# The last two dK stores of a cached-attention backward kernel, each as sixteen transfers of 8 partitions

## The chip, the core and the metric

The kernel runs on one core of a Trainium2 chip. A core has four compute engines (PE for matmuls, DVE for elementwise work, ACT, POOL), a fifth one, SP, that does nothing here but issue transfers, and sixteen DMA engines, which move all data between HBM and the on-chip memory of 128 partitions. The metric is the device time of one execution in microseconds, as the median of several runs.

## The reference

What is computed is a decoding step with its gradients: layer norm, attention over a cache of 4,096 keys and values for 4 x 32 heads, a gated MLP, and the derivative by eight of the inputs. Cut to what matters here:

```python
B, Sq, D = 4, 1, 512
H, Sk, Dh = 32, 4096, 128
"k_cache": (B, H, Sk, Dh), "v_cache": (B, H, Sk, Dh)      # bf16
...
q = ((x @ wq).reshape(B, Sq, H, Dh)).transpose(0, 2, 1, 3)
scores = jnp.einsum("bhqd,bhkd->bhqk", q, k_cache) * (Dh ** -0.5)
p = softmax(scores)
o = jnp.einsum("bhqk,bhkd->bhqd", p, v_cache)
...
_out, _vjp = jax.vjp(_f, A_x, A_k_cache, A_v_cache, A_wq, A_wo, B_w1, B_w3, B_w2)
return (_out, *_vjp(grad_out))
```

With one query per head, the gradient of a head's values is an outer product, dV = p dO^T, and that of its keys is dK = dS q^T, with dS the gradient of the scores. Each is 4,096 x 128 numbers in bf16, 1 MiB a head. The caches are read (K once, V twice) and two arrays of their size are written, which makes up nearly all of the 705 MB that the kernel moves.

## The kernel before

**Stages.** The forward part goes through the 128 heads with K and V. The backward part then goes through them again with V alone. Its first 32 heads are done one by one, the other 96 in 48 pairs (`NT = 48`; `t` is the pair). A pair is two heads side by side: each head takes 64 partitions, and each partition holds 64 rows of 128 numbers, 16,384 bytes that are contiguous in HBM as well (`two_heads`, L1272).

**One pair.** `load_pair` (L1276) loads V, `front_pair` (L1292) transposes it on PE and ACT and multiplies it with dO, `group_dS_pair` (L1319) makes dS, and `grad_pair` (L1386) makes and stores one result: it takes a pair of slots, lets DVE write the outer product into it (`outer_pair`, the instruction at L1379), has SP store it (L1389), and gives the slots back. dV (`out_3`) comes from `more_V` (L1395), which runs ahead by some heads, and dK (`out_2`) from the loop over `t` at the end of the kernel. So the last stores of the program, in SP's order, are dV and dK in turn, then dV of the last pair, dK of pair `NT-2`, dK of pair `NT-1`. There is no load behind them.

**Slots.** All these tiles are pieces of one on-chip tile, `arena`, of 23 slots; `Slot2` (L146) takes two neighbouring ones, those that were given back longest ago. The program's dependencies are found by the framework from the pieces that each instruction reads and writes; the order of instructions on each engine is the order in the source.

**The queue.** SP runs its list in order. An instruction that waits holds up all behind it. Every transfer of SP's counts up one of eight semaphores, which the framework hands out in turn, so a semaphore comes back with every eighth transfer. In the built program each transfer waits for what it reads or overwrites, and also until the earlier transfer of its own semaphore has landed in full: all its parts, on all DMA engines. In the program of before, the last two dK stores wait, besides DVE's product, for the eighth transfer before each.

**A landing** is the time at which the last of a transfer's sixteen parts (one for each DMA engine) has been counted. A 128-row store of a pair puts 8 rows, so 8 packets of 16,384 bytes, on each DMA engine.

Of the kernel before, what the change touches and what calls it, by code (L numbers as in the profile page):

```python
# [27 lines left out]
def kernel(  # L28
# [22 lines left out]
    nc = tc.nc  # L51
# [6 lines left out]
    Dh = A_k_cache.shape[3]  # L58
# [6 lines left out]
    SJ = Sk // P  # L65
# [142 lines left out]
    for i in range(2):  # L208
        t = fcon.tile([P, 64], BF16, name=f"onesw{i}")
# [4 lines left out]
    def ones_window(col):  # L214
# [11 lines left out]
                          in_=rowg[:, None, :, None].to_broadcast([P, 4, 8, 4]))  # L226
# [738 lines left out]
    with ExitStack() as c2:  # L965
# [297 lines left out]
        NT = (NH - SP) // 2  # L1263
# [8 lines left out]
        def two_heads(ap, t):  # L1272
            b, h = t % B, H0 + t // B * 2
            return ap[b, h:h + 2].rearrange("h (p j) d -> (h p) (j d)", p=P // 2)
# [103 lines left out]
        def outer_pair(dst, col2, row):  # L1378
            nc.vector.tensor_tensor(  # L1379
                out=dst.rearrange("p (j r t) -> p j r t", r=Dh // 2, t=2),  # L1380
                in0=col2[:, :, None, :].to_broadcast([P, 2 * SJ, Dh // 2, 2]),
                in1=row.rearrange("p (r t) -> p r t", t=2)[:, None, :, :].to_broadcast([P, 2 * SJ, Dh // 2, 2]),
                op=ALU.mult,
            )

        def grad_pair(out_ap, t, col2, row):  # L1386
            g_ = Slot2()
            outer_pair(g_.t[:, 0:2 * SJ * Dh], col2, row)
            nc.sync.dma_start(out=two_heads(out_ap, t), in_=g_.t[:, 0:2 * SJ * Dh])  # L1389
            g_.give()  # L1390

        O0, S0, S1, L, LP = 2, 21, 35, 5, 3
        gvd = {"n": 2, "t": 0}
# [1 line left out]
        def more_V(upto):  # L1395
            while gvd["n"] < min(SP, upto):
                s = gvd["n"]
                P_pairs(s)
                replicate("rdo", s - s % REP)
                grad_V(s)  # L1400
                P_pairs(s + 1)
                P_pairs(s + 2)
                gvd["n"] += 1
                if s % REP == 2 and s + 2 < SP:
                    replicate("rdo", s + 2)
                elif s % REP == 2:
                    replicate_pair("rdo", 0)
                if s >= SP - 2:
                    P2_pair(s - SP + 2)
            while gvd["t"] < NT and SP + 2 * gvd["t"] + 2 <= upto:  # L1410
                t = gvd["t"]
                P2_pair(t)
                replicate_pair("rdo", t // B)
                grad_pair(out_3, t, pP2.pop(t), reps["rdo", "p", t // B][:, t % B, :])
                P2_pair(t + 1)
                gvd["t"] += 1
                if t % B == 2:
                    replicate_pair("rdo", t // B + 1)
# [57 lines left out]
        for t in range(NT):  # L1476
            s = SP + 2 * t
            load_pairs(t + LP)
            if t % B == 2:
                replicate_pair("rq", t // B + 1)  # L1480
            if t + LP < NT:
                front_pair(t + LP, lambda: side(s))
            else:
                if t + LP == NT:
                    rows_out()
                    rows_T()
                side(s)
            more_V(s + 2 + lead_V(s))
            grad_pair(out_2, t, pdS[t // 2][:, t % 2], reps["rq", "p", t // B][:, t % B, :])
            if t % 2 == 1 and t + 1 < NT:  # L1490
                group_dS_pair((t + 1) // 2)
            side(s + 1)
# [31 lines left out]
```

## Time and profile before

| what | value |
|---|---|
| median of 3 runs | 1698.76 us (1698.05 to 1699.05) |
| span of the profiled execution | 1696.2 us |
| moved by DMA | 707.45 MB, mean 417 GB/s |
| DVE, PE, ACT, POOL busy | 1234.4, 1233.4, 959.5, 336.9 us |
| 2,048 KB stores (dV and dK of pairs) | 96, median 27.9 us from issue to landing |
| outer product of a pair on DVE (L1379) | 4.42 us |
| last dV store: issued, landed | 1658.14, 1685.22 us |
| dK store of pair NT-2: issued, landed | 1662.52, 1690.05 us |
| dK store of pair NT-1: issued, landed | 1666.81, 1694.89 us |

Times within the execution count from its first instruction. Busy times are sums over the span, and engines run side by side, so they don't add up to it. The time from issue to landing is mostly queueing: several stores stand in the queues at a time. The profiled execution's span is 2.6 us less than the median of the runs, which count a little before and behind it.

### The profile page before, as it was taken

The numbers are of one execution on the slowest core, as the hardware profiler recorded it, in microseconds if no ns is written. First come the engines' busy times: TensorE is split into PE (matmuls) and PEld (weight loads), VectorE is DVE, ScalarE is ACT, GpSimd is POOL, SyncE is SP. The second block draws the span as 40 slices with busy tenths as digits, with TensorE's granted clock in tenths as the row PEclk, the third lists the DMA queues.
The fourth block names the chain that finished last, engine by engine and source line by source line (L and its number), as shares of the span: only waits on it lengthen the run. The fifth ranks groups of instructions, "written<-read, shape, count | busy, mean of one in ns | idle before, by whom it ended". The sixth has DMA issues, their size and how long they took to land.

```text
span 1696.2 us, 37839 instructions
## 1 busy us (share of the span) xinstructions
PE 1233.4 (73%) x16228; PEld 943.4 (56%) x16228; DVE 1234.4 (73%) x1198; ACT 959.5 (57%) x1490; POOL 336.9 (20%) x583
## 2 busy tenths in 40 slices
PE   5889888888888888877876755667665666766650
PEld 4777667666677666655655544444444444444440
DVE  5989999999998997667766466575665655655683
ACT  3555544454454544677665555666665666666650
POOL 1211222222222222222231121011210102011120
PEclk8999999999999999899898689886678777676675
DMA  9999999999999999999999999999999999999995
GB/s 401 424 424 424 424 424 424 424 424 423 416 423 406 424 414 397 395 414 425 425 425 429 428 429 428 429 430 429 429 429 428 418 430 429 422 418 425 415 429 230
DMA packets 81000, 707.45 MB, mean 417 GB/s; under 512 B 8748, under 2 KB 12984, under 8 KB 15296
## 3 DMA queue, kind: packets, MB, share of 16 engines
q1 hardware_dynamic: 80416, 704.94, 99.0%
q8 instruction: 127, 2.08, 0.5%
q14 instruction: 41, 0.34, 0.0%
q0 software_dynamic: 416, 0.10, 0.0%
HBM read 422.59 MB, written 282.34 MB: 416 GB/s over the span
## 4 chain that ended last, share of the span: by engine, by line
DMA 46%; DVE 9%; PE 3%; issue 2%; ACT 1%; DVEq 0%; POOL 0%; SPq 0%; ACTq 0%
DMA out_dram<-arena 43%; DVE arena L1379 7%; DMA arena<-in_A_v_cache_dram 3%; DVE arena L806 1%; PE M_ps L472 1%; DVE arena L457 1%; PE pt_w L601 0%; ACT arena L1299 0%; ACT Pn L436 0%; DVEq L1519 0%; PE kP_ps L482 0%; DVE dPr L1326 0%; PE pt_tps L1298 0%; PE gu_ps L873 0%; PE dn_ps L904 0%
## 5 line engine op out<-in xcount | busy, mean ns | idle before, releaser
L1299 ACT COPY arena<-pt_tps 128x1024 bf16<-128x1024 bf16 x384 | 369.8, 1023 | 232.3 <-PE pt_tps L1298 231.6
L1298 PE MATMUL pt_tps<-ident_b,arena 128*128 128x128 bf16 x3072 | 308.1, 272 | 204.7 <-DMA arena<-in_A_v_cache_dram 149.4
L1298 PEld LDWEIGHTS <-arena 128*128 128x128 bf16 x3072 | 263.9, 125 | 304.2 <-DMA arena<-in_A_v_cache_dram 172.8
L1379 DVE TENSOR_TENSOR arena<-arena 128x8192 bf16<-128x8192 bf16 x48 | 212.5, 4427 | 205.1 <-DMA out_dram<-arena 202.3
L472 PE MATMUL M_ps<-arena 128*128 128x130 bf16 x4096 | 285.1, 222 | 42.9 <-DMA arena<-in_A_v_cache_dram 42.2
L457 DVE TENSOR_TENSOR arena<-arena 128x4096 bf16<-128x4096 bf16 x128 | 292.5, 2285 | 23.9 <-POOL arena L453 23.9
L472 PEld LDWEIGHTS <-arena 128*128 128x128 bf16 x4096 | 251.9, 99 | 64.0 <-DMA arena<-in_A_v_cache_dram 57.2
L1379 DVE TENSOR_TENSOR arena<-dS,arena 128x8192 bf16<-128x8192 bf16 x48 | 212.3, 4424 | 73.0 <-DMA out_dram<-arena 73.0
L364 DVE STREAM_TRANSPOSE arena<-arena 128x512 f32<-128x512 f32 (+1 forms) x321 | 250.7, 797 | 0.0
L359 ACT COPY arena<-pt_tps 128x1024 bf16<-128x1024 bf16 x128 | 129.5, 1012 | 188.9 <-PE pt_tps L358 150.5
L1376 POOL COPY arena<-arena 128x128 bf16<-128x128 bf16 x48 | 55.3, 1153 | 492.3 <-ACT arena L1353 286.3
L370 POOL TENSOR_TENSOR W<-qrep,wmask 128x128 bf16<-128x128 bf16 x128 | 120.2, 939 | 85.6 <-PE S_ps L390 70.8
L801 ACT COPY arena<-pt_tps 128x1024 bf16<-128x1024 bf16 x128 | 121.7, 1025 | 26.1 <-PE pt_tps L800 24.8
L453 POOL COPY arena<-P_all 128x64 bf16<-128x64 bf16 x128 | 32.7, 255 | 412.8 <-ACT P_all L447 409.8
L806 DVE TENSOR_TENSOR arena<-dS,arena 128x4096 bf16<-128x4096 bf16 x32 | 73.2, 2293 | 35.0 <-DMA out_dram<-arena 34.7
L800 PE MATMUL pt_tps<-ident_b,arena 128*128 128x128 bf16 x1024 | 78.5, 229 | 27.1 <-ACT arena L801 27.1
L1313 PE MATMUL dP_ps<-arena 128*32 128x512 bf16 x768 | 85.7, 484 | 7.6 <-ACT arena L1299 7.3
L800 PEld LDWEIGHTS <-arena 128*128 128x128 bf16 x1024 | 67.2, 104 | 37.5 <-issue 35.9
L447 ACT COPY P_all<-pt_P 32x64 bf16<-32x64 bf16 x256 | 52.1, 204 | 53.6 <-PE pt_P L443 51.4
L806 DVE TENSOR_TENSOR arena<-P,arena 128x4096 bf16<-128x4096 bf16 x29 | 66.4, 2295 | 19.8 <-DMA out_dram<-arena 19.8
L358 PE MATMUL pt_tps<-ident_b,arena 128*128 128x128 bf16 x1024 | 80.1, 222 | 0.0
L482 PE MATMUL kP_ps<-arena,onesw 128*32 128x512 bf16 x1024 | 79.6, 388 | 0.0
(245 smaller groups left out, 1576.5 us busy)
## 6 DMA issues: line engine op xcount, KB each, us to landing
out_dram<-arena SPq DMA_DIRECT2D x96, 2048.0 KB, 27.9
arena<-in_A_v_cache_dram SPq DMA_DIRECT2D x160, 1024.0 KB, 15.9
arena<-in_A_k_cache_dram SPq DMA_DIRECT2D x128, 1024.0 KB, 15.3
arena<-in_A_v_cache_dram SPq DMA_DIRECT2D x48, 2048.0 KB, 32.1
out_dram<-arena SPq DMA_DIRECT2D x72, 1024.0 KB, 20.2
arena<-in_A_wq_dram SPq DMA_DIRECT2D x8, 1024.0 KB, 14.4
arena<-in_B_w_dram SPq DMA_DIRECT2D x8, 896.0 KB, 15.3
out_dram<-arena SPq DMA_DIRECT2D x6, 896.0 KB, 28.4
```

Of the source, the lines that this page charges most:

```text
L359: nc.scalar.copy(out=KT[:, c * GW:(c + 1) * GW, :], in_=pt[:])
L364: nc.vector.transpose(out=KT[:, c * w_:(c + n) * w_], in_=Kn[:, c * w_:(c + n) * w_])
L370: nc.gpsimd.tensor_tensor(out=W[:, hl], in0=qrep[:, :, s:s + 1].to_broadcast([P, 4, 32]), in1=wmask[:, hl, None, :].to_broadcast([P, 4, 32 ...
L457: nc.vector.tensor_tensor(out=PK[:, :, 0:Dh].rearrange("p j (r t) -> p j r t", t=2), in0=Ks[s].heads().rearrange("p j (r t) -> p j r t", t=2),
L472: nc.tensor.matmul(hold["M"][:], lhsT=Vn[:, j, :], rhs=PK[:, j, :], start=(j == 0), stop=(j == SJ - 1))
L800: nc.tensor.transpose(pt[:, i, :], v[:, g * GW + i, :], ident_b[:])
L801: nc.scalar.copy(out=v[:, g * GW:(g + 1) * GW, :], in_=pt[:])
L806: nc.vector.tensor_tensor(out=dst.rearrange("p j (r t) -> p j r t", t=2), in0=col2[:, :, None, :].to_broadcast([P, SJ, Dh // 2, 2]), in1=r ...
L1298: nc.tensor.transpose(pt[:, i, :], v[:, g * GW + i, :], ident_b[:])
L1299: nc.scalar.copy(out=v[:, g * GW:(g + 1) * GW, :], in_=pt[:])
L1313: nc.tensor.matmul(rows["acc"][32 * c:32 * (c + 1), :], lhsT=zt[t % B][:, 32 - m:64 - m], rhs=v[:, j0:j0 + 4, :], start=(pl == 0 and u == ...
L1379: nc.vector.tensor_tensor(out=dst.rearrange("p (j r t) -> p j r t", r=Dh // 2, t=2), in0=col2[:, :, None, :].to_broadcast([P, 2 * SJ, Dh / ...
```

## The change

`grad_pair` hands its store to a new function. For every dV and for dK of the pairs up to `NT-3` that function issues the same transfer as before. For dK of the last two pairs it issues sixteen transfers each: a transfer takes the 8 partitions `o, o+4, ..., o+28` of a group of 32, for four values of `o` in each of the four groups. The eight transfers of the lower half (partitions 0 to 63) go out at once. Those of the upper half (64 to 127) are held back, for both pairs, until the lower half of the last pair is out. The slots of these two results are not given back. What is computed, and by which engine, is the same.

```diff
         def grad_pair(out_ap, t, col2, row):
             g_ = Slot2()
             outer_pair(g_.t[:, 0:2 * SJ * Dh], col2, row)
-            nc.sync.dma_start(out=two_heads(out_ap, t), in_=g_.t[:, 0:2 * SJ * Dh])
-            g_.give()
+            store_pair(two_heads(out_ap, t), g_.t[:, 0:2 * SJ * Dh], t, out_ap is out_2)
+            if out_ap is out_3 or t < NT - 2:
+                g_.give()
+
+        held = []
+
+        def store_pair(dst, src, t, is_k):
+            if not is_k or t < NT - 2:
+                nc.sync.dma_start(out=dst, in_=src)
+                return
+            held.append((dst, src))
+            for b0 in (0, 32):
+                for o in range(b0, b0 + 4):
+                    nc.sync.dma_start(out=dst[o:o + 29:4, :], in_=src[o:o + 29:4, :])
+            if t == NT - 1:
+                for dst, src in held:
+                    for b0 in (64, 96):
+                        for o in range(b0, b0 + 4):
+                            nc.sync.dma_start(out=dst[o:o + 29:4, :], in_=src[o:o + 29:4, :])
```

## Prediction

> **What bounds the kernel now.** I read the page first: its line of DMA shares, in 40 slices of 42.4 us.
>
> ```profile
> span 1696.2 us, 37839 instructions
> DMA  9999999999999999999999999999999999999995
> GB/s 401 424 424 424 424 424 424 424 424 423 416 423 406 424 414 397 395 414 425 425 425 429 428 429 428 429 430 429 429 429 428 418 430 429 422 418 425 415 429 230
> ```
>
> The sixteen DMA engines are full from beginning to end, and only the last slice is half empty. So nothing that computes sets the time; the transfers do, and what can still be won or lost lies in the last slice. The same view in narrow stretches (per stretch: busy time of each engine, then clock, DMA share, GB/s):
>
> ```profile
> 1664.00:1675.00 11.00, 0.00 (x0) 0.00 (x0) 2.79 (x1) 0.00 (x0) 0.00 (x0) 0.50 0.97 413
> 1675.00:1677.00 2.00, 0.00 (x0) 0.00 (x0) 0.00 (x0) 0.00 (x0) 0.00 (x0) 0.50 0.40 172
> 1677.00:1679.00 2.00, 0.00 (x0) 0.00 (x0) 0.00 (x0) 0.00 (x0) 0.00 (x0) 0.50 0.06 25
> 1679.00:1694.60 15.60, 0.00 (x0) 0.00 (x0) 0.00 (x0) 0.00 (x0) 0.00 (x0) 0.50 0.06 26
> ```
>
> A share of 0.06 is 1/16: from 1677.6 us on, one DMA engine alone still moves data, 26 GB/s for 17 us. The sixteen completion marks of the last store say the same: seven at 1674.6 to 1674.9 us, eight at 1676.6 to 1677.6, one at 1694.9. I call it the laggard. It is late with every store near the end: the last eight (dK and dV in turn) have all but one mark 17 us before their landing. The instructions of line 1389, for the last store alone:
>
> ```profile
> L1389 SPq DMA_DIRECT2D out_dram<-arena x1: 333/333/333, 1666.8 to 1666.8; - x1
> DMA to landing us min/median/max: 28.1/28.1/28.1
> ```
>
> Issued at 1666.81, landed at 1694.89. Then the waits of SP's queue (who waited for whom: us in total, times, longest) and the end of the chain of waits:
>
> ```profile
> SPq L1519 <- DMA out_dram<-arena: 27.6, 2, 22.8
> ```
> ```profile
> 1653.70 4.42 DVE arena L1379
> 1658.12 4.34 DVEq L1519
> 1662.45 4.33 DVE arena L1379
> ```
>
> DVE makes the last two dK tiles, 1658.03 to 1662.45 and on to 1666.78; SP issues each 0.07 us later, and then only waits for the landings.
>
> **The change, step by step.** It takes the two 128-row stores away (2 x 4.86 us on every DMA engine: 8 rows of 16,384 bytes, one packet of 0.611 us each, starting 0.607 us apart, plus a completion mark of 0.006 us) and issues 32 transfers of 8 rows. I number them #1 to #8 (lower half, t = NT-2), #9 to #16 (lower half, t = NT-1) and #17 to #32 (the upper halves).
>
> The instruction lists of the two built programs show two waits that the diff doesn't. First, SP's transfers use eight semaphores in turn, and each waits until the transfer eight before it has landed in full, laggard included. So #1 to #8 wait for the last eight 128-row stores, which landed at 1651.1, 1656.1, 1660.9, 1665.8, 1670.7, 1675.5, 1680.4 and 1685.2 us. Before, only the first two of these were waited for, and had long passed. Now #8 can't be issued until 1685.22. Second, DVE's last instruction (line 1379, the dK tile of NT-1) waited for one store; now it waits for eight counts, those that #1 to #8 complete. The tile takes a partition-strided access for one that overlaps it. Behind that DVE instruction stands #9, and behind #9 on SP the other 23.
>
> The sum, from 1685.22 us, the landing of the last dV store. Nothing before 1662.5 us differs, so it stands:
> - Issue of #8, 0.02 us (what SP took after a landing in the final waits: 1690.053 to 1690.070).
> - From issue to first packet: SP's first load is issued at 0.74 us and its first packet starts at 1.77, so 1.03 us. That is the one row with an idle queue; bounds 0.33 us (the issue itself, 332 ns) and 1.03; I take 1.03, the only one seen whole.
> - The row, 0.61 us, and its mark to the landing 0.40 us (last store: mark at 1694.49, landing at 1694.89). Landing of #8: 1687.28.
> - DVE: 0.03 us and the product, 4.43 us. This product lay under the transfers before; its cover is gone. Ends at 1691.74.
> - #9: 0.07 + 1.03 us. First packet at 1692.84.
> - Rows #9 to #32. No transfer under 128 rows goes through SP in this trace, so how 8 rows are shared is bounded. In the 128-row stores each engine has 8 whole-row packets. One row on each of eight engines: 0.607 + 0.006 = 0.613 us a transfer. From below, rows halved over all sixteen (the 8,192-byte loads take 0.309 us): then SP's issue decides, 0.378 us from one issue to the next wait (1662.516 to 1662.895). From above, all eight on one engine, 4.9 us. I take 0.613, since the stores of the trace show rows in whole packets and shares that are equal; 24 x 0.613 = 14.71 us, to 1707.55.
> - Mark to landing 0.40, and the closing 0.91 us after the eighth semaphore's wait (1695.27 to 1696.18). Span 1708.86.
>
> Against 1696.18 that is +12.7 us; the median of the runs is 1698.76, 2.6 us above the profiled span, so 1711.4 us, +0.75%.
>
> Terms of nothing: 30 more issues on SP cost 0.378 us each under rows of 0.613. The longer hold of one slot pair costs nothing, no later tile takes it. PE, ACT and POOL have no work after 1651.9 us and get no new waits. #1 to #7 go out as the semaphores come and lie wholly under the laggard.
>
> Does the pipeline of 24 hold? Eight may be in flight, one alone takes 1.03 + 0.61 + 0.40 = 2.04 us, eight rows take 4.9, so the engines shouldn't run dry. The Trainium skill speaks against the change here ("DMA: Bandwidth & Descriptors", sections "Anatomy of one DMA — SWDGE (gpsimd) path" and "Rules for kernel authors"): a transfer has a fixed cost near 2.0 us plus bytes over 436 GB/s, and one should use 128 partitions and 1 MiB or more. By that price, paid 24 times in a row, 2.3 us each, this stage would take about 55 us instead of 14.7; no run here shows it.
>
> Another page rule bears on the laggard (same page, "Latency and other measured facts"): engines 7 and 15 are usually the slower ones. The trace has one laggard, without its number; if only eight engines carry the small rows, the page leaves open whether it is one of them.
>
> **The rivals.**
> - *The laggard is among the eight* that carry the rows. Then #8's row waits behind #1 to #7 on it: 1684.76 + 8 x 0.613 + 0.40 = 1690.07 instead of 1687.28. That is +2.8, 1714.2 us. For or against it nothing speaks in the trace; for the forecast I take the end without the term.
> - *Rows are halved over sixteen engines.* #8 lands 0.30 earlier, DVE ends at 1691.44, the last issue is at 1691.44 + 0.07 + 23 x 0.378 = 1700.20, the end 1.03 + 0.31 + 0.40 + 0.91 later: 1702.9, +6.7, 1705.5 us. Against it: no store in the trace has packets under a row.
> - *Small transfers overlap poorly*, two instead of eight at once: 1.02 us each, 24 x 0.41 = 9.8 more, 1721.2 us. For it: SP's transfers of before move 56 KB or more per engine, so the trace can't show small ones side by side.
> - *Faster: the laggard is relieved in time.* If neither wait binds, SP puts all 32 in the queues by about 1677 us, and the laggard is rid of its last 16 rows: 1694.89 - 9.73 = 1685.2. The eight carriers get 16 rows more: 1677.6 + 9.73 + 0.18 = 1687.5, end 0.91 later, -7.8 us, 1691.0 us. It decides if #8 is issued before about 1677 us. Against it stands the landing at 1685.2 of the store that #8 waits for.
> - *The change has nothing to relieve*, since the lag is absent when it runs. Then the dV store lands at 1667.9, #8 at 1672.8, DVE ends at 1677.3, the rest adds 1.1 + 14.7 + 1.3: 1694.4, -1.8 us, 1697.0 us, no change. Against it: the code ahead is the same, and the runs of before lie within 1 us.
>
> **How the numbers follow.** Chances: forecast 0.48, laggard among the eight 0.25, halved rows 0.07, poor overlap 0.12, relieved in time 0.04, no lag 0.04. The time is the forecast's, 1711.4. From 1705 to 1717 us lie the first three, 0.80; left out are the other three, and the price of all rows on one engine (over 100 us), which no equal share supports. A measurement of this kernel tells about 0.2% (3.4 us) from no change: faster 0.04, the same 0.04, slower 0.92.
>
> **What would show it.** In the new profile: SP waits from 1667 to 1685 us, in steps of 4.9 us, for landings of the big stores; DVE is idle until about 1687 us and then runs one last product of 4.4 us; the DMA share is 0.06 to about 1684.8, near nothing to 1692.8, then 0.50 for 14.7 us. A share of 1.0 in the last stretch would mean sixteen carriers, one far below 0.5 poor overlap. An early last product, at 1662 us, would make the prediction wrong; so would a laggard that is gone.

## The result and the profile after

| | before | after |
|---|---|---|
| median of 4 runs each | 1698.54 us (1698.05 to 1699.05) | 1715.14 us (1714.58 to 1715.72) |
| ratio, 95% interval | 1 | 1.0100 (1.0087 to 1.0113) |
| span of the profiled execution | 1696.2 us | 1713.9 us |
| landing of the last dV store | 1685.22 us | 1685.83 us |
| end of DVE's last product | 1666.78 us | 1695.27 us |
| last row's completion mark | 1694.49 us | 1712.65 us |

The change costs 16.6 us, 1.0%. The page of after, its span and its DMA lines:

```profile
span 1713.9 us, 37874 instructions
DMA  9999999999999999999999999999999999999992
GB/s 401 424 424 424 424 423 425 424 423 422 419 424 408 424 412 397 374 424 424 425 427 427 429 429 429 430 430 429 429 429 426 420 429 428 423 420 425 419 393 96
```

Up to the last two slices little has changed; the last one moves 96 GB/s where it moved 230. The same end in narrow stretches of after (busy time of PE, PE's weight loads, DVE, ACT, POOL, then clock, DMA share, GB/s):

```profile
1664.00:1675.00 11.00, 0.00 (x0) 0.00 (x0) 0.00 (x0) 0.00 (x0) 0.00 (x0) 0.50 0.37 159
1675.00:1685.00 10.00, 0.00 (x0) 0.00 (x0) 0.00 (x0) 0.00 (x0) 0.00 (x0) 0.50 0.12 51
1685.00:1690.00 5.00, 0.00 (x0) 0.00 (x0) 0.00 (x0) 0.00 (x0) 0.00 (x0) 0.50 0.12 49
1690.00:1692.00 2.00, 0.00 (x0) 0.00 (x0) 1.16 (x1) 0.00 (x0) 0.00 (x0) 0.50 0.00 0
1692.00:1695.00 3.00, 0.00 (x0) 0.00 (x0) 3.00 (x1) 0.00 (x0) 0.00 (x0) 0.50 0.00 0
1700.00:1712.00 12.00, 0.00 (x0) 0.00 (x0) 0.00 (x0) 0.00 (x0) 0.00 (x0) 0.50 0.46 194
```

Read the DMA share from above. In the first stretch it falls from 0.97 before to 0.37, as the two big stores are no longer there. To 1690 us the laggard works nearly alone. In the next two stretches nothing moves at all, while DVE makes the last product, and then eight engines of sixteen work, 0.46. The timeline of after shows the same from the instructions (start, length, engine, line; in brackets how long the engine had been idle, and what ended that):

```profile
1658.61 4.42 DVE L1379 TENSOR_TENSOR arena<-dS,arena 128x8192 bf16<-128x8192 bf16 x1
1658.72 0.33 SPq L1397 DMA_DIRECT2D out_dram<-arena  x1
1663.18 37.44 SPq L1402 DMA_DIRECT2D out_dram<-arena  x16
1690.84 4.42 DVE L1379 TENSOR_TENSOR arena<-dS,arena 128x8192 bf16<-128x8192 bf16 x1 [27.81 <-DMA out_dram<-arena]
1700.66 10.67 SPq L1407 DMA_DIRECT2D out_dram<-arena  x16
```

Two dK products that ran back to back before now stand 27.81 us apart, and a DMA ended that wait. The issues themselves, from the list of lines 1402 and 1407 of after (duration in ns, least, median and most; first and last start):

```profile
L1402 SPq DMA_DIRECT2D out_dram<-arena x16: 625/625/775, 1663.2 to 1700.0; - x16
```
```profile
L1407 SPq DMA_DIRECT2D out_dram<-arena x16: 625/625/626, 1700.7 to 1710.7; - x16
```

From #9 on, SP issues one transfer every 0.669 us: 625 ns for the issue and 0.044 us to the next. And SP's waits in the last 60 us of after, with the end of its chain of waits:

```profile
SPq L1402 <- DMA out_dram<-arena: 17.9, 5, 4.2
SPq L1402 <- DVE arena L1379: 12.7, 2, 8.7
```
```profile
1654.28 4.43 DVE arena L1379
1658.72 27.11 DMA out_dram<-arena
1685.85 4.87 DMA out_dram<-arena
1690.84 4.42 DVE arena L1379
```

The chain is the predicted one: the last dV store (27.11 us), then #8 (4.87 us from issue to landing), then the product. The five waits of 4.2 us at most are #4 to #8, issued at 1666.40, 1671.29, 1676.14, 1680.99 and 1685.85 us, each just behind the landing of a big store.

What the DMA packets of after show besides: every small transfer is eight packets of 16,384 bytes, one on each of eight engines, and seven of these eight start their row of #8 between 1687.12 and 1687.19 us. The eighth still has the big stores to do, and runs its rows of #1 to #8 one after the other from 1685.38 to 1690.28 us. So the laggard is among the eight.

The laggard's last mark moved by 18.2 us (1694.49 to 1712.65). Of this 9.8 are the 16 more rows that it carries now (it had 2 x 8, it has 32; 16 x 0.613). It stands idle for 6.3 us from 1690.28 to the first packet of #9 at 1696.57. Its last 24 rows are 0.669 us apart instead of 0.613: 1.35. The last dV store landed 0.6 later. These sum to 18.05. The medians differ by 16.6 us only: the profiled execution of after, 1715.72 us, is the slowest of its four, and that of before, with a span of 1696.2 us, is at the fast end of its own.

### The profile page after: what moved, and what is told of

It reads as the page before. It is cut to its first block, busy times and chain, and to the rows that moved or that the text cites. A ratio compares the mean times of both kernels' runs of the same rounds, so it can differ in the third digit from the quotient of the medians.

```text
span 1713.9 us, 37874 instructions
## 1 busy us (share of the span) xinstructions
PE 1234.0 (72%) x16228; PEld 946.2 (55%) x16228; DVE 1234.2 (72%) x1198; ACT 958.6 (56%) x1490; POOL 340.4 (20%) x583
## 4 chain that ended last, share of the span: by engine, by line
DMA 41%; DVE 9%; PE 6%; ACT 5%; issue 2%; POOL 0%; SPq 0%; DVEq 0%; ACTq 0%
DMA out_dram<-arena 39%; DVE arena L1379 7%; ACT arena L801 4%; DMA arena<-in_A_v_cache_dram 2%; PE dq_ps L1000 1%; PE pt_tps L800 1%; PE dP_ps L1228 1%; DVE arena L806 1%; PE M_ps L472 1%; DVE arena L457 1%; PE pt_wo L610 1%; PE pt_w L601 0%; ACT arena L1299 0%; ACT Pn L436 0%; PE kP_ps L482 0%
```

## The experiments

All variants compute the same outputs as the kernel; only how the last two dK stores are issued differs. Ratios are to runs of the kernel before on the same chip. The diffs are against the changed kernel, inside `store_pair`, unless another base is named.

**Rows that lie together, the same counts and order.** This takes away the strided access that makes DVE wait.

```diff
-            for b0 in (0, 32):
-                for o in range(b0, b0 + 4):
-                    nc.sync.dma_start(out=dst[o:o + 29:4, :], in_=src[o:o + 29:4, :])
+            for o in range(0, 64, 8):
+                nc.sync.dma_start(out=dst[o:o + 8, :], in_=src[o:o + 8, :])
...
-                    for b0 in (64, 96):
-                        for o in range(b0, b0 + 4):
-                            nc.sync.dma_start(out=dst[o:o + 29:4, :], in_=src[o:o + 29:4, :])
+                    for o in range(64, P, 8):
+                        nc.sync.dma_start(out=dst[o:o + 8, :], in_=src[o:o + 8, :])
```

> Undoes one part: the 8 partitions of a transfer lie together instead of 4 apart; number, size and order of the transfers stay. The built program's last DVE product then waits for one old store again, not for #1 to #8. Theory (two waits in a row: the semaphores hold SP until the last dV store lands near 1685.8 us, then DVE's last product waits for #8): DVE's product runs near 1663 us, SP still waits until 1685.8, then #9 to #32 follow #8 at once, 24 x 0.669 us, end about 2.3 + 0.9 us after the last issue: span 1705.1, time near 1707, so 8 to 9 us under the changed kernel and still 8 us over before. Rival A (the eight carriers' own work is the cost, the DVE wait costs nothing): span stays near 1713.9. Rival B (only the DVE wait costs, the semaphores do not): 1690 or less. Also: SP's issue stays 0.625 us if few rows are the cause of it, and falls to 0.33 us if the stride is.

Measured: 1724.48 us (1723.36 to 1724.96), ratio 1.0155 (1.0140 to 1.0170). A miss, in the unexpected direction. The timeline of this variant and two stretches of it:

```profile
1657.26 8.75 DVE L1379 TENSOR_TENSOR arena<-dS,arena 128x8192 bf16<-128x8192 bf16 x2
1661.74 36.62 SPq L1401 DMA_DIRECT2D out_dram<-arena  x16
1698.41 18.88 SPq L1405 DMA_DIRECT2D out_dram<-arena  x16
```
```profile
1675.00:1690.00 15.00, 0.00 (x0) 0.00 (x0) 0.00 (x0) 0.00 (x0) 0.00 (x0) 0.50 0.28 44
1690.00:1720.00 30.00, 0.00 (x0) 0.00 (x0) 0.00 (x0) 0.00 (x0) 0.00 (x0) 0.50 0.43 107
```

DVE's wait is gone: both products run back to back from 1657.26 us. What was won is lost, and more, in the rows. In the last stretch the engines are busy for 0.43 of the time and move 107 GB/s; in after they were busy for 0.46 and moved 194. An engine's row takes 0.43 x 16 x 16,384 bytes / 107 GB/s = 1.05 us on the mean here and 0.62 there, and single packets took up to 4.6 us (from 1680.7 us). The Trainium skill has a rule that fits ("SBUF — State Buffer", section "Door 1: The DMA port swizzle (why `[64,N]` ≈ `[32,N]`)"): four neighbouring partitions lie on one port, so eight neighbours reach two ports, and eight that are 4 apart reach eight. The rows agree, 0.61 us at 4 apart and 1.05 on the mean together. That the ports are the reason is argued and not shown, since the addresses in HBM move with the partitions. So the stride that costs DVE's wait buys the speed of the rows. It also costs issue time: an issue of eight rows that met no backlog took 0.276 us together and 0.625 us at 4 apart.

**All 32 transfers behind the last product.** The transfers, their rows and their order are those of the change; only DVE no longer stands between #8 and #9.

```diff
-            for b0 in (0, 32):
-                for o in range(b0, b0 + 4):
-                    nc.sync.dma_start(out=dst[o:o + 29:4, :], in_=src[o:o + 29:4, :])
             if t == NT - 1:
-                for dst, src in held:
-                    for b0 in (64, 96):
-                        for o in range(b0, b0 + 4):
-                            nc.sync.dma_start(out=dst[o:o + 29:4, :], in_=src[o:o + 29:4, :])
+                for lo in (0, 64):
+                    for dst, src in held:
+                        for b0 in (lo, lo + 32):
+                            for o in range(b0, b0 + 4):
+                                nc.sync.dma_start(out=dst[o:o + 29:4, :], in_=src[o:o + 29:4, :])
```

> The transfers are exactly those of the changed kernel, 4 apart, in the same order, but all 32 are issued after DVE's last product, so that no product stands behind a small transfer. Theory: the same as with the rows together, span 1705.1, time near 1707, for the DVE wait is gone and the semaphores stay. Rival (the stride itself, not the wait it brings, is slow): 1711 or more while the rows together give 1707.

Measured: 1707.52 us (1707.18 to 1708.66), ratio 1.0057 (1.0042 to 1.0072), as expected. Three stretches of this variant and SP's waits at its end:

```profile
1676.00:1686.00 10.00, 0.00 (x0) 0.00 (x0) 0.00 (x0) 0.00 (x0) 0.00 (x0) 0.50 0.12 49
1686.00:1704.20 18.20, 0.00 (x0) 0.00 (x0) 0.00 (x0) 0.00 (x0) 0.00 (x0) 0.50 0.44 184
1704.20:1705.60 1.40, 0.00 (x0) 0.00 (x0) 0.00 (x0) 0.00 (x0) 0.00 (x0) 0.50 0.06 23
```
```profile
SPq L1405 <- DMA out_dram<-arena: 13.6, 4, 4.2
SPq L1405 <- DVE arena L1379: 8.3, 1, 8.3
```

The product's turn costs 1715.14 - 1707.52 = 7.6 us, or 1.0100 - 1.0057 = 0.43% of 1698 = 7.3 us by the ratios. The rest, 0.57% or 9.7 us, stays. In the last stretch one engine is busy alone, 0.06: seven carriers end at 1704.1 us, the laggard at 1705.44. Its row stream has no gap from the big stores to the end. So two bounds lie close together here: SP, which waits for #8 until 1686.10 us and then issues every 0.669 us (to 1702.17), and the laggard, which has 16 rows more to do. The laggard ends 1.3 us after the others, but without its 16 rows SP's pace would have left an end nearly as late. So this run can't tell which of the two the rest belongs to; a later one does.

**Sixteen rows a transfer**, also behind the last product, so that all sixteen engines share again.

```diff
...
-                    for b0 in (64, 96):
+                    for b0 in (0, 64):
                         for o in range(b0, b0 + 4):
-                            nc.sync.dma_start(out=dst[o:o + 29:4, :], in_=src[o:o + 29:4, :])
+                            nc.sync.dma_start(out=dst[o:o + 61:4, :], in_=src[o:o + 61:4, :])
```

> The same small pieces on all sixteen engines: eight transfers of 16 partitions (4 apart) for each of the two stores, issued after the last product, so that no DVE wait comes in and the rows are shared as before, 8 a store on each engine. Theory: the laggard has the rows it had before and its queue never runs dry (#1 to #7 stand in it when SP gets past the landing at 1685.2 us), so span 1696 to 1697, time within 1 us of before. Rival (small transfers cost by themselves, 0.67 us each in series): 9 of them behind 1685.8 us plus 3 us, still hidden, so it would show in SP's rows alone. Rival (small transfers stall the engines): 3 us or more above before. SP's issue: 0.625 us if a small transfer or the stride is the cause, near 0.33 us if it is that fewer than sixteen engines take part.

Measured: 1700.84 us (1699.13 to 1701.36), ratio 1.0015 (1.0006 to 1.0024). With sixteen carriers nearly all of the 9.7 us is gone, though SP still waits for its semaphores up to the landing of the last dV store (half as many transfers stand behind that). The 3 us that are left and that were not expected are again in the rows: most took 0.7 to 1.2 us, and in the last ten microseconds the median was 1.19, twice 0.611. By the rule on ports above, sixteen partitions 4 apart within a half of 64 lie in pairs on eight ports, which agrees. Its issues took 0.49 to 0.59 us where the queue let them, so an issue is dear because of the stride, not because few engines take part.

**Shares of seven.** Each of the last two stores as 119, 7 and 2 partitions that lie together. The packets show seven engines with 17 rows of the 119, and one row each of the 7; nothing of these falls on the eighth. The question is whether the laggard is that eighth.

```diff
-            held.append((dst, src))
...
+            for o, n in ((0, 119), (119, 7), (126, 2)):
+                nc.sync.dma_start(out=dst[o:o + n, :], in_=src[o:o + n, :])
```

> Asks which engine the laggard is, and lifts the semaphore wait at once: each of the last two dK stores goes out as three transfers of 119, 7 and 2 partitions, six in all, which wait for stores landed by 1675.5 us. The 8-row transfers had eight carriers, the laggard among them. If 119 rows go in seven shares of 17 to seven of these eight, and the laggard is the eighth: it ends near 1685.2 us with the dV store, the seven carriers have 37 rows more from about 1664.9 us, 1687.5, span 1688.8, time near 1691, 0.45% under before. If the laggard is one of the seven: it gets 37 rows instead of 16, 1694.9 + 21 x 0.607 = 1707.6, time near 1711. If the rows are shared in another way (16 carriers): near before, 1698. The Trainium skill (DMA: Bandwidth & Descriptors, section on the semaphore's increment of 16) gives the number of carriers as the largest up to 16 that divides the rows, on the lowest-numbered engines, which makes it 7 here.

Measured: 1716.74 us (1715.64 to 1717.90), ratio 1.0110 (1.0093 to 1.0127). The laggard is among the first seven: it ends alone, with the 36 rows that one of the seven has (2 x 18). The time is some 6 us above the 1711 expected for this case. That lies ahead of these rows: the last dV store landed at 1691.44 us instead of 1685.22, behind a stretch in which rows took longer (0.75 us on the mean of all engines from 1665 to 1680 us, 0.61 before). From there the 36 rows take 0.61 us each, but for one. The last stretch of this variant has a share of 0.07, one engine in sixteen:

```profile
1697.00:1714.00 17.00, 0.00 (x0) 0.00 (x0) 0.00 (x0) 0.00 (x0) 0.00 (x0) 0.50 0.07 28
```

**Which of the seven?** The last dK store alone, as 112, 8, 4, 2 and 2 partitions (NT-2 stays one transfer):

```diff
-            held.append((dst, src))
...
+            if t < NT - 1:
+                nc.sync.dma_start(out=dst, in_=src)
+                return
+            for o, n in ((0, 112), (112, 8), (120, 4), (124, 2), (126, 2)):
+                nc.sync.dma_start(out=dst[o:o + n, :], in_=src[o:o + n, :])
```

> Prices a row on the laggard with no wait in the way, and narrows down which engine it is. Only the last dK store differs from the kernel before: it goes out as five transfers of 112, 8, 4, 2 and 2 partitions, whose semaphores are free by 1680.4 us. The laggard gets 7 rows of the 112 instead of 8, then a row of each later transfer that it carries. Theory (the changed kernel's end is set by the rows that the laggard gets; it is one of the first seven): each row costs it 0.61 us; with one more row (of the 8) it ends as before, near 1694.9 us; with two (8 and 4) 0.6 us later, with four 1.8 us later; span 1696.2, 1696.8 or 1698.0, time 1698 to 1700. In the packets the single stream at the end shows which. Rival (the wait, not the rows): none of these transfers waits past 1680.4 us, so the end would come with the other engines' last row or with the 7 rows alone, 1694.3, 0.6 us earlier than before.

Measured: 1700.75 us (1700.31 to 1701.63), ratio 1.0016 (1.0007 to 1.0026). The laggard's last packets are the seven rows of the 112 (1692.2 to 1696.5 us) and then one more, not three or four. So it takes part in a transfer of 8 and in none of 4 or 2. The price of a row did not come out as expected: with 16 rows, as many as before, the laggard's last one ends 2.65 us later. Of this 2.2 us are there when the last dV store lands, at 1687.40 us, and most of the rest is in two later rows of the laggard that took 0.89 and 0.69 us. So 0.61 us a row is the price while the laggard works alone; beside other transfers a row can take longer.

The same with 112, 6, 5 and 5 (the line that differs from the variant above, without its case for `t < NT - 1`):

```diff
-            for o, n in ((0, 112), (112, 8), (120, 4), (124, 2), (126, 2)):
+            for o, n in (((0, 128),) if t < NT - 1 else ((0, 112), (112, 6), (118, 5), (123, 5))):
```

> Narrows the laggard down: the transfers of 112 partitions and of 8 gave it a row or more, the one of 4 gave it none, and those of 119 gave it its share, so it is the fifth, sixth or seventh carrier. Only the last dK store differs from before: 112, 6, 5 and 5 partitions. The single stream at the end has the 7 rows of the 112 and then 3 more (fifth), 1 more (sixth) or none (seventh): the last row near 1696.1, 1694.9 or 1694.3 us. If it isn't the same engine in each run, another count would turn up.

Measured: 1701.64 us, a single run, so its time is read no closer than that. Behind the seven rows of the 112 came three more packets on the laggard, at 1696.56, 1697.19 and 1697.80 us: it takes part in the 6 and in both of 5. If a transfer of k rows uses the first k engines of one fixed order, the laggard is among the first five, and as transfers on four engines don't use it (the 4 of the variant above, and the 116 of a run below on the same chip as this one), it is the fifth. The runs stand on several chips; none of their counts speaks against this place.

**POOL's queue instead of SP's.** The 32 transfers of the second experiment, issued by POOL, whose order of issue knows nothing of SP's semaphores (diff against that experiment).

```diff
-                                nc.sync.dma_start(out=dst[o:o + 29:4, :], in_=src[o:o + 29:4, :])
+                                nc.gpsimd.dma_start(out=dst[o:o + 29:4, :], in_=src[o:o + 29:4, :])
```

> The 32 transfers of 8 rows of the products-first kernel, issued by POOL instead of SP: they count on eight other semaphores, so no transfer waits for a store of SP's, and no product waits. If the eight semaphores behind the old stores were the cost (theory of the prediction, with the laggard not in the way): end near 1688 to 1692 us, time 1690 to 1694. If the laggard's own rows are the cost and the carriers are the same eight: 32 rows instead of 16 on it, 1694.9 + 9.8 = 1704.7, time near 1707. If POOL's transfers are shared over all sixteen in turn: 16 rows on the laggard, as before, time near 1699. POOL's issue of a transfer may cost more than SP's 0.67 us; at 1 us each the last goes out at 1699, end near 1702. The Trainium skill (DMA: Bandwidth & Descriptors, section on the semaphore's increment of 16) says that POOL's transfers of fewer parts move on round the sixteen engines, which would make it the third case.

Measured: 1709.70 us (1709.18 to 1710.14), ratio 1.0070 (1.0053 to 1.0087). POOL's part of the timeline, cut after the first three lines, and a stretch at its end:

```profile
1666.89 4.12 POOL L1405 DMA_DIRECT2D out_dram<-arena  x8 [23.94 <-DVE arena L1379]
1672.85 0.52 POOL L1405 DMA_DIRECT2D out_dram<-arena  x1 [1.84 <-DMA out_dram<-arena]
1674.70 0.52 POOL L1405 DMA_DIRECT2D out_dram<-arena  x1 [1.33 <-DMA out_dram<-arena]
```
```profile
1703.00:1704.40 1.40, 0.00 (x0) 0.00 (x0) 0.00 (x0) 0.00 (x0) 0.00 (x0) 0.50 0.06 23
```

Twenty of the transfers are out by 1692 us, where SP in the second experiment had issued some sixteen, and #8 is out by 1671 instead of at 1686. It gains nothing. The same eight engines carry all 32. The laggard alternates packet by packet between SP's big stores and POOL's small ones, so the dV store lands later, at 1692.85 us, and the laggard ends, again without a gap, at 1704.3. That is its end before plus sixteen rows: 1694.49 + 9.8 = 1704.3. This settles the question of the second experiment as far as the engine goes: without any product in the way and without SP's semaphores, the eight carriers' extra rows on the laggard alone set an end some 10 us late. POOL has its own waits for landings (13 times, 16.1 us in all), so it is no run without any such wait; but the laggard's rows follow one another without a gap, all 32 of POOL's among them, so these waits did not set its end. The span ends 3.1 us after the laggard's last row, about 1.5 us more than before, which is most of what the time has above these 9.8.

**Can the laggard be relieved?** Two variants use carriers without it, for NT-2 only (the last store is one transfer): 116 + 12 partitions, four engines for the first, and 92 + 32 + 4.

```diff
-            held.append((dst, src))
...
+            for o, n in (((0, 116), (116, 12)) if t < NT - 1 else ((0, 128),)):
+                nc.sync.dma_start(out=dst[o:o + n, :], in_=src[o:o + n, :])
```
```diff
+            for o, n in (((0, 92), (92, 32), (124, 4)) if t < NT - 1 else ((0, 128),)):
```

> A version to gain by it: the dK store of pair NT-2 goes out as 116 partitions (29 rows on each of four carriers, the laggard not among them) and 12 (one row on twelve), the last one as before. The laggard has 9 rows after the dV store instead of 16: 1685.2 + 9 x 0.607 = 1690.7 us. The four carriers have 29 + 1 + 8 rows from 1664.9 us: 1688.0, plus up to 7 rows slowed from 0.61 to 1.2 us where two of them read partitions of one port: 1692. Span 1692 to 1693.5, time 1694.5 to 1696, 0.15 to 0.25% under before. If the rows don't set the end: no difference.

> The same with less on the four carriers: 92 partitions (23 rows each), then 32 over all sixteen (2 rows each) and 4; the last store as before. The laggard has 10 rows after the dV store: 1691.3 us; the carriers 23 + 2 + 1 + 8 rows from 1664.9: 1685.5, or some us more where rows meet at a port. Span 1692.6, time 1695, 0.2% under before.

Measured: 1697.48 us, ratio 0.9997 (0.9988 to 1.0006), and 1696.70 us, ratio 0.9993 (0.9984 to 1.0002). Neither can be told from the kernel before. Rows took longer (in the first many took 0.8 to 1.7 us and a few up to 4.6), and the dV store, which the laggard still has to finish, landed at 1688.95 and 1687.65 us instead of 1685.22: what the laggard is spared at the end it loses to slower rows ahead.

The third takes the lower 64 partitions of both stores as one transfer each from SP, and the upper 64 from POOL as sixteen transfers of 4 rows for each store, 4 apart, in which the laggard has no part.

```diff
-            for b0 in (0, 32):
-                for o in range(b0, b0 + 4):
-                    nc.sync.dma_start(out=dst[o:o + 29:4, :], in_=src[o:o + 29:4, :])
+            nc.sync.dma_start(out=dst[0:64, :], in_=src[0:64, :])
...
-                    for b0 in (64, 96):
+                    for b0 in range(64, P, 16):
                         for o in range(b0, b0 + 4):
-                            nc.sync.dma_start(out=dst[o:o + 29:4, :], in_=src[o:o + 29:4, :])
+                            nc.gpsimd.dma_start(out=dst[o:o + 13:4, :], in_=src[o:o + 13:4, :])
```

> Another version to gain by it, free of what spoiled the last two (rows that meet the laggard at a port of the on-chip memory, and a landing of the dV store 2 to 4 us later for it): of both last dK stores the lower 64 partitions go out from SP as one transfer, 4 rows on each engine, and the upper 64 from POOL as sixteen transfers of 4 partitions, 4 apart, after the last product. If four rows have four carriers on POOL's queue too, and the laggard isn't one of them, it has 8 rows after the dV store: 1685.2 + 8 x 0.613 = 1690.1 us; the four carriers have 32 + 4 rows from 1668: 1690.1. Span 1691.5, time 1693 to 1694, 0.25 to 0.3% under before. If POOL's small transfers move on round the engines, the laggard gets 8 more, as before: time near 1698. If the rows of the laggard are not what sets the end, or POOL's issue of 0.52 us grows to 0.8 us: the last goes out at 1693.6, 1696 to 1698.

Measured: 1710.40 us (1709.87 to 1711.22), ratio 1.0073 (1.0059 to 1.0087), a miss by 17 us. The first lines of POOL's part of the timeline of this variant:

```profile
1666.87 4.11 POOL L1405 DMA_DIRECT2D out_dram<-arena  x8 [23.95 <-DVE arena L1379]
1683.83 2.56 POOL L1405 DMA_DIRECT2D out_dram<-arena  x5 [12.85 <-DMA out_dram<-arena]
```

The rows of the first eight transfers ran from 1674.2 to 1679.3 us on four engines, but the first transfer landed only at 1683.55 us, and POOL's ninth issue waited 12.85 us for that. A transfer of POOL's counts marks from all sixteen engines. The late marks of the first one are not the laggard's, whose packets put its mark at 1677.86 us. They are those of two other engines, which have none of POOL's rows and ran SP's rows of the 64-partition stores, at 2.4 us each, until 1681.9 and 1683.0 us. From the ninth transfer on the laggard's mark comes last: the other fifteen of that transfer are counted by 1686.25 us, its own at 1690.04. So an engine that carries none of the rows holds a transfer up, and here first the slow rows of the 64 partitions and then the laggard's backlog did so. This run relieved the laggard of rows (its last was over at 1697.43 us) and lost that to waits of another kind; it doesn't show what carriers without the laggard would give if nothing waited for it.

## Why the prediction was right, and where it was off

The direction, the two waits and the range held: 1715.14 us lies in 1705 to 1717, 3.7 above the 1711.4 that was forecast. By its own steps:

- *SP waits for eight semaphores, so #8 goes out at the landing of the last dV store.* Shown: #4 to #8 each left at a landing, #8 at 1685.85 us. The step's start, 1685.22, came 0.6 later, which is within what executions differ by.
- *DVE's last product waits for #1 to #8, #9 for the product.* Shown by the timeline (27.81 us idle), and the second experiment, which takes only this away, puts 7.3 to 7.6 us on it. Its 4.43 us was 4.42.
- *The laggard's place.* This is the step that failed. The forecast took "the end without the term", 0 us; the term was there. On the laggard #8's row stands behind seven others and ends at 1690.28 us, where the forecast had 1686.88 (its landing at 1687.28 less 0.40). Of these 3.4 us 0.6 are the later start; the rest is the +2.8 of the rival *the laggard is among the eight*, whose 1714.2 us is nearest to the measured time. The trace of before did not hold the answer; the packets of after do, and the shares of 116, 6 and 5 put it in the fifth place of the carriers.
- *Issue to first packet, 1.03 us.* For #9 it was 1.27 (1695.30 to 1696.57), +0.24.
- *24 x 0.613.* A size: the rows were right (one whole row on each of eight engines, 0.613 to 0.618 us), but the price of an issue was not. "cost 0.378 us each under rows of 0.613" came from a 128-row store; eight rows 4 apart took 0.625, with 0.044 to the next 0.669. So SP set the pace, 24 x 0.669 = 16.06 us, +1.35.

Together 0.6 + 2.8 + 0.24 + 1.35 = 5.0, which is the difference of the spans, 1713.9 less 1708.86. The forecast of the time is only 3.7 off, and that is luck: the median of after lies 1.2 above its profiled span, and 2.6 had been added. That 2.6 is a median less the span of a fast execution; in the runs whose own span is listed the time lies 1.8 above it (1715.72 and 1713.9).

The rivals: *rows halved over sixteen* and *poor overlap* are out, since every transfer is eight whole rows and they follow each other every 0.669 us, not 1.02. *No lag* is out, since the laggard was there in every trace. *The laggard is relieved in time* was wrong in its price and not only in its condition. It gave -7.8 us, on the ground that the eight carriers and the laggard are different engines. They are not: the change takes 16 rows off the eight engines that carry no small ones and lays 16 more on the one engine that sets the end. The runs without the product's wait, with SP (the second experiment) and with POOL, in both of which the laggard's rows follow one another without a gap, end at +9.7 and +11.9 us (0.57% and 0.70% of 1698). So even with both waits mended this change would have made the kernel slower, and no case of the prediction said so.

The Trainium skill's price of 2.3 us a transfer (about 2.0 fixed, which the page measured on POOL's path), by which the last 24 in a row would have taken 55 us, holds here for one transfer and not for the row: #9 took 2.29 us from its issue at 1695.30 to its landing at 1697.59, but all 24 took 16 us, with several in flight at a time. Its page "DMA: Bandwidth & Descriptors", section "Why a DMA increments its semaphore by 16 and not by 1", says how many engines take part, the largest number up to 16 that divides the slowest dimension, and for SP's kind of queue the lowest-numbered ones. The packets agree with the number in each case (8 rows on eight, 119 on seven, 116 on four). By the second part the laggard, the fifth, would be engine 4, not 7 or 15, the ones that the prediction had named from that page; no trace here gives the engines' numbers. For POOL's queue that section has the group of engines move on round the sixteen from transfer to transfer, and here it did not: all 32 transfers of 8 rows ran on the same eight, and those of 4 on the same four.

What stays open is why this engine lags. In before the last mark of a transfer of SP's comes on the mean under 0.4 us behind the fifteenth until 800 us, 4 us behind it in the 900s, when the pair stores begin, and 17 us from 1600 us on. From 1000 to 1560 us the last marks come 5.01 to 5.06 us apart (medians) and the fifteenth ones 4.85. But the last eight stores land 4.84 to 4.88 us apart, and the laggard's rows in them take 0.611 us like the others': at the end it is late, not slow. The packets that could be told apart don't show what else it does.

## What to carry to other kernels

Before a transfer is split to relieve the queues, find which DMA engine ends last and whether the pieces fall on it: pieces with fewer rows than engines went to a fixed few here (and so did 119 and 116 rows, to seven and four), and those of five to eight rows, like the 119, held the one late engine. Then look at the built program for what the pieces wait for, above all a semaphore that comes back every eighth transfer and a producer that takes a strided piece for an overlap, and price an issue by its own shape. Where one engine lags 17 us, what must wait for a full landing takes the lag over. On POOL's queue that holds even for a store that has none of its rows there; on SP's it did not: the piece of 4 rows issued at 1668.12 us in the 112, 8, 4, 2 and 2 landed at 1679.16 us, where that of 8 landed at 1697.47.

## What the runs showed of the hardware

- An issue on SP took 0.332 us for 128 rows, 0.354 for 119, 0.276 for 8 rows together, 0.236 for 2, but 0.625 for 8 rows 4 apart and 0.49 to 0.59 for 16 rows 4 apart, each where the queue held it up least.
- A row of 16,384 bytes took 0.611 to 0.620 us in transfers of eight rows 4 apart, mostly 0.7 to 1.2 in those of sixteen rows 4 apart, and 1.05 on the mean, up to 4.6, in those of eight rows that lie together.
- One DMA engine, by these runs the fifth of those that SP's transfers use, was 17 us late at the end of a span of 1,700 us.
- A POOL transfer with rows on four engines landed only when busy engines that had none of them had counted their marks: the first, with its rows over at 1675.0 us, at 1683.55; the ninth, counted by fifteen engines at 1686.25 us, at 1690.04 with the laggard's mark.
